# Running the last block of rows of a spectral-mixing and SwiGLU kernel as two half blocks, with the closing stores on two DMA queues

## The chip, the cores and the metric

One Trainium2 chip, one core. The metric is the device time of one launch in microseconds, lower is better. A kernel of 904 us is looked at for an effect of about 1 us. Two lengths are used throughout, both read from a trace:

- **S**: from the start of the first gate matmul of the last block of rows to the start of its last gate matmul (a step's gate is two matmuls; the first of the two is meant);
- **C**: from there to the end of the span.

S + C is all that the change can touch.

The names in the traces: PE runs the matmuls, ACT (ScalarE) the silus, DVE (VectorE) the multiplies (both also copy results), and SP, at the end, only issues stores. PSUM holds the sums of the matmuls, in pieces called banks. A semaphore is a counter that one engine raises and another waits for; a store's completion semaphore tells that its data has landed.

## The reference

In short form:

```python
def reference(x, filt_r, filt_i, w_gate, w_val, w_out, rms_g):   # x: 8 x 3008 x 256, float32
    X = np.fft.rfft(x, axis=1)
    y = np.fft.irfft(X * (filt_r + 1j * filt_i)[None], n=3008, axis=1)
    t = y.reshape(24064, 256)
    tn = t / np.sqrt(np.mean(t * t, axis=-1, keepdims=True) + 1e-6) * rms_g
    g = tn @ w_gate                                              # 256 -> 1536
    return ((g / (1 + np.exp(-g))) * (tn @ w_val)) @ w_out       # 1536 -> 256
```

## The kernel before

The spectral part of a batch runs under the SwiGLU part of the batch before it. The last batch has nothing left to overlap, so the end is SwiGLU alone: for each block of 512 rows, twelve steps (`jt`). A step has four 512-column matmuls (gate and value), a silu on ACT, a multiply on DVE and, two steps later, four 256-column matmuls that add the step's share to the output accumulators. After the twelfth step ACT copies one accumulator bank out of PSUM, DVE the other, and SP issues the stores.

```python
    def gv(b, m, jt):                       # one step: gate, value, silu, multiply
        w = nq(b, m) * P                    # 512 columns
        ...
        for ps, wt in ((pg, wg), (pv, wv)):
            for dt_ in range(2):
                nc.tensor.matmul(ps[:, 0:w], wt[:, dt_, ts(jt, P)], xn[:, dt_, 0:w], ...)
        nc.scalar.activation(out=sg[:, 0:w], in_=pg[:, 0:w], func=AXT.Silu)
        nc.vector.tensor_tensor(out=hh[:, 0:w], in0=pv[:, 0:w], in1=sg[:, 0:w], op=ALU.mult)

    def down(b, m, jt):                     # two steps later
        ...                                 # po: two accumulators, one PSUM bank each
        for s4 in range(n):
            nc.tensor.matmul(po[s4 // 2][:, s4 % 2, :], hh[:, ts(s4, P)], wo[:, jt, :], ...)
        if jt == JT - 1:
            nc.scalar.activation(out=o3[:, 0:2, :], in_=po[0], func=AXT.Copy)
            nc.vector.tensor_copy(out=o3[:, 2:n, :], in_=po[1][:, 0:n - 2, :])

    def o_store(b, m):                      # the last block: 256, 192 and 64 KB
        for h in range(2):
            w = 3 if (m == 5 and (h or b % 2 == 0)) else 4
            lo = h * H + 4 * m
            nc.sync.dma_start(rows[:, lo:lo + w, :], o3[h * 64:h * 64 + 64, 0:w, :])
        if m == 5 and b % 2:                # 64 rows of the batch before ride along
            nc.sync.dma_start(prev[:, H - 1, :], o3[64:P, 3, :])
```

## Time and profile before

| kernel before | |
|---|---|
| time, median of the first three runs | 904.32 us (904.30 to 905.29) |
| span of the profiled run | 903.3 us |
| PE busy | 97% of the span |
| S, C, S + C | 14.52, 8.13, 22.64 us |

Two lines of the page, the busy times and the shares of the chain that ended last:

```profile
PE 878.7 (97%) x6329; PEld 561.0 (62%) x6329; DVE 676.9 (75%) x1075; ACT 619.3 (69%) x1047; POOL 391.4 (43%) x353
...
PE 86%; issue 5%; DMA 3%; DVE 2%; POOL 2%; ACT 2%; SPq 0%; POOLq 0%; ACTq 0%
```

PE bounds the kernel; a change at the end can win only what stands after PE has run dry. That end, from the timeline (start, duration, engine, line, operation, tiles; in brackets the idle time before and what ended it):

```profile
895.65 0.59 PE L420 MATMUL pv<-xn,wv 128*128 128x512 f16 x2
895.85 0.60 ACT L424 ACTIVATE sg<-pg 128x512 f16<-128x512 f32 x1 [0.70 <-PE pg L420]
...
896.08 1.76 PE L437 MATMUL po<-wo,hh 128*128 128x256 f16 x12
896.47 0.69 DVE L425 TENSOR_TENSOR hh<-pv,sg 128x512 f16<-128x512 f32 x1 [0.61 <-ACT sg L424]
...
897.65 0.60 ACT L442 ACTIVATE o<-po 128x512 f32<-128x512 f32 x1 [1.21 <-PE po L437]
897.87 0.69 DVE L443 COPY o<-po 128x512 f32<-128x512 f32 x1 [0.71 <-PE po L437]
898.63 1.11 SPq L452 DMA_DIRECT2D out_dram<-o  x2
899.78 0.61 SPq L456 DMA_DIRECT2D out_dram<-o  x1
```

Three store issues stand in a row until 900.39. The remaining 2.9 us to 903.3 hold no compute. A DMA's line here is only its issue. The Trainium skill, "Perfetto Trace Analysis", section "DMA Instruction — HWDGE (DVE, Sync)", says that the moving of the data lies outside the reported window; this trace agrees, since the third store, issued at 899.785, landed (its completion semaphore's last step in the trace) at 902.355. What SP waits for at the end, from the view of the waits (total us, times, longest):

```profile
SPq L800 <- DMA out_dram<-o: 1.5, 3, 0.9
SPq L800 <- PEq L800: 0.7, 2, 0.5
```

### The profile page before, as it was taken

What the parts mean: (1) busy time and instruction counts of PE and PEld (TensorE: products, weight loads), DVE (VectorE), ACT (ScalarE), POOL (GpSimd) and SP (SyncE); (2) the same over time, 40 slices, a digit from 0 to 9 for tenths busy, and PEclk for the clock granted to TensorE, in tenths of its full rate; (3) what the DMA queues carried; (4) which work ended last, traced back from release to release, by engine and by line L of the source; (5) the groups of instructions that cost most, each with busy time, mean ns of one, the idle gap of its engine ahead of it and who ended that gap; (6) DMA issues with size and microseconds to landing.
All of it is one profiled execution on the core that took longest, in us unless ns stands there. A gap on an engine that the chain in (4) does not pass through costs nothing.

```text
span 903.3 us, 17520 instructions
## 1 busy us (share of the span) xinstructions
PE 878.7 (97%) x6329; PEld 561.0 (62%) x6329; DVE 676.9 (75%) x1075; ACT 619.3 (69%) x1047; POOL 391.4 (43%) x353
## 2 busy tenths in 40 slices
PE   8689999999999999999999999999999999999997
PEld 5565666666666666666666666666666666666564
DVE  7756767789887887888788886887878887555554
ACT  8657666677677766877667766787657765676443
POOL 7832740555635552465325552265514552043300
PEclk9799999999999999999999999999999999999999
DMA  9495734774664437444554347243252332321201
GB/s 199 82 182 159 144 76 164 166 171 79 165 168 116 90 72 213 106 95 113 135 147 111 88 96 193 81 105 82 74 173 71 65 88 54 97 70 48 60 24 46
DMA packets 79747, 100.91 MB, mean 112 GB/s; under 512 B 8097, under 2 KB 56417, under 8 KB 79277
## 3 DMA queue, kind: packets, MB, share of 16 engines
q1 hardware_dynamic: 69276, 83.45, 33.8%
q0 software_dynamic: 10384, 16.35, 11.4%
q8 instruction: 49, 0.80, 0.4%
q14 instruction: 38, 0.30, 0.1%
HBM read 67.67 MB, written 46.78 MB: 127 GB/s over the span
## 4 chain that ended last, share of the span: by engine, by line
PE 86%; issue 5%; DMA 3%; DVE 2%; POOL 2%; ACT 2%; SPq 0%; POOLq 0%; ACTq 0%
PE po L437 25%; PE pg L420 25%; PE pv L420 25%; PE psi L286 3%; PE psb L241 3%; PE psn L318 2%; DMA fr<-in_filt_r_dram 2%; PE psa L204 2%; PE psq L339 1%; DVE o L443 1%; DMA rb<-r_tmp 1%; POOL xc L189 0%; DVE hh L425 0%; ACT fr L478 0%; ACT sg L424 0%
## 5 line engine op out<-in xcount | busy, mean ns | idle before, releaser
L425 DVE TENSOR_TENSOR hh<-pv,sg 128x512 f16<-128x512 f32 (+1 forms) x576 | 391.4, 680 | 203.6 <-ACT sg L424 88.9
L424 ACT ACTIVATE sg<-pg 128x512 f16<-128x512 f32 (+1 forms) x576 | 338.8, 588 | 231.1 <-PE pg L420 223.1
L437 PE MATMUL po<-wo,hh 128*128 128x256 f16 x2256 | 342.3, 272 | 2.3 <-DVE o L443 1.6
L420 PE MATMUL pv<-xn,wv 128*128 128x512 f16 (+1 forms) x1152 | 337.9, 375 | 0.0
L420 PE MATMUL pg<-xn,wg 128*128 128x512 f16 (+1 forms) x1152 | 337.9, 375 | 0.0
L437 PEld LDWEIGHTS <-hh 128*128 128x128 f16 x2256 | 216.5, 98 | 99.2 <-issue 3.6
L277 POOL TENSOR_TENSOR s<-s,s 128x512 f16<-128x512 f16 x96 | 110.5, 1151 | 285.5 <-DVE s L271 199.5
L420 PEld LDWEIGHTS <-wv 128*128 128x128 f16 x1152 | 112.7, 98 | 131.2 <-issue 0.6
L403 POOL TENSOR_TENSOR xn<-y,rb 128x1024 f16<-128x1024 f32 (+1 forms) x45 | 126.1, 2802 | 46.7 <-DMA rb<-r_tmp 32.8
L420 PEld LDWEIGHTS <-wg 128*128 128x128 f16 x1152 | 109.2, 98 | 12.3 <-issue 0.3
L345 POOL TENSOR_TENSOR rho<-u,mhalf 128x4 f32<-128x4 f32 (+1 forms) x48 | 48.9, 1018 | 85.6 <-DVE u L343 85.6
L291 ACT ACTIVATE t<-psi 96x512 f16<-96x512 f32 x112 | 66.3, 592 | 11.8 <-PE psi L286 6.3
L324 ACT ACTIVATE y<-psn,gsb 128x512 f32<-128x512 f32 (+1 forms) x94 | 63.8, 678 | 10.1 <-PE psn L318 3.0
L271 DVE TENSOR_TENSOR s<-psb,fi 64x512 f16<-64x512 f32 x96 | 65.7, 684 | 3.0
L273 DVE SCALAR_TENSOR_TENSOR s<-psb,fi 64x512 f16<-64x512 f32 x96 | 66.5, 693 | 1.3
L247 DVE TENSOR_TENSOR s<-psb,fr 128x512 f16<-128x512 f32 x96 | 65.4, 681 | 0.0
L330 ACT ACTIVATE sq<-psn 128x512 f16<-128x512 f32 (+1 forms) x94 | 54.8, 583 | 0.0
L209 ACT ACTIVATE t<-psa 128x512 f16<-128x512 f32 x70 | 41.8, 597 | 5.6 <-PE psa L204 2.4
L286 PE MATMUL psi<-s,wi 128*128 128x256 f16 x248 | 45.4, 273 | 0.0
L241 PE MATMUL psb<-t,wb 96*128 96x256 f16 x224 | 43.0, 272 | 0.9 <-DVE s L264 0.9
L286 PEld LDWEIGHTS <-wi 128*128 128x128 f16 x248 | 24.2, 98 | 27.0 <-issue 1.9
L318 PEld LDWEIGHTS <-t 128*128 128x128 f16 x368 | 28.5, 99 | 19.9
(97 smaller groups left out, 515.7 us busy)
## 6 DMA issues: line engine op xcount, KB each, us to landing
out_dram<-o SPq DMA_DIRECT2D x84, 256.0 KB
xc<-in_x_dram POOLq DMA_DIRECT2D x56, 192.0 KB, 6.4
z_tmp<-t SPq DMA_DIRECT2D x28, 384.0 KB
t<-z_tmp SPq DMA_DIRECT2D x28, 384.0 KB
g_tmp<-t SPq DMA_DIRECT2D x56, 192.0 KB
rb<-r_tmp SPq DMA_DIRECT2D x41, 256.0 KB
t<-g_tmp SPq DMA_DIRECT2D x21, 384.0 KB
out_dram<-o SPq DMA_DIRECT2D x12, 192.0 KB
```

What stands on the lines that cost most here:

```text
L241: nc.tensor.matmul(ps[:, u, :], w[:, k, :], t, start=True, stop=True)
L247: nc.vector.tensor_tensor(out=s1, in0=ps, in1=f1, op=ALU.mult)
L271: nc.vector.tensor_tensor(out=s2[a], in0=ps[e], in1=f2[e], op=ALU.mult)
L273: nc.vector.scalar_tensor_tensor(out=s2[a], in0=ps[e], scalar=-1.0, in1=f2[e], op0=ALU.mult, op1=ALU.mult)
L277: nc.gpsimd.tensor_tensor(out=s, in0=s1, in1=s2, op=ALU.add)
L286: nc.tensor.matmul(ps[:, u, :], wi_at(q, 2 * i + u), ss[q][:, u, :], start=(q == 0), stop=(q == n - 1))
L291: nc.scalar.activation(out=st[b]["t3"][c][:, 2 * r:2 * r + 2, :], in_=ps[0:KR], func=AXT.Copy)
L403: nc.gpsimd.tensor_tensor(out=xv, in0=yv, in1=rv.unsqueeze(1).to_broadcast([P, 2, n, P]), op=ALU.mult)
L420: nc.tensor.matmul(ps[:, 0:w], wt[:, dt_, ts(jt, P)], xn[:, dt_, 0:w], start=(dt_ == 0), stop=(dt_ == 1))
L424: nc.scalar.activation(out=sg[:, 0:w], in_=pg[:, 0:w], func=AXT.Silu)
L425: nc.vector.tensor_tensor(out=hh[:, 0:w], in0=pv[:, 0:w], in1=sg[:, 0:w], op=ALU.mult)
L437: nc.tensor.matmul(po[s4 // 2][:, s4 % 2, :], hh[:, ts(s4, P)], wo[:, jt, :], start=(jt == 0 and s4 % 2 == 0), stop=(jt == JT - 1 and (s4 ...
```

## The change

The intent is to shorten the tail. The last block runs as two halves of 256 columns, 24 half steps instead of 12. The first half's stores go out under the second half, the second half's chain is shorter, and only 256 KB are left to store at the end, one store of it on ACT's queue beside SP's two.

```diff
-    def gv(b, m, jt):
-        w = nq(b, m) * P
-        xn = st[b]["xn"][m]
+    def cut(b, m, part):
+        return (0, nq(b, m)) if part is None else (2 * part, 2)
+
+    def gv(b, m, jt, part):
+        q0, n = cut(b, m, part)
+        w = n * P
+        xn = st[b]["xn"][m][:, :, q0 * P:q0 * P + w]
 ...
-            po_of[(b, m)] = [psO.tile([P, 2, D], FP32, tag="po%d" % i, name="po%d" % i)
-                             for i in range(2)]
+            po_of[(b, m, part)] = [psO.tile([P, 2, D], FP32, tag="po%d" % i, name="po%d" % i)
+                             for i in range(2) if part is None or i == part]
 ...
+            else:
+                nc.scalar.activation(out=o3[:, 0, :], in_=po[0][:, 0, :], func=AXT.Copy)
+                nc.vector.tensor_copy(out=o3[:, 1, :], in_=po[0][:, 1, :])
 ...
+        if part is not None:
+            lo = 4 * m + 2 * part
+            for h, eng in ((0, nc.scalar), (1, nc.sync)):
+                w = 2 - h * part
+                eng.dma_start(rows[:, h * H + lo:h * H + lo + w, :], o3[h * 64:h * 64 + 64, 0:w, :])
+            if part:
+                prev = ...
+                nc.sync.dma_start(prev[:, H - 1, :], o3[64:P, 1, :])
+            return
 ...
-        items = [(b, m, jt) for b in range(B) for m in range(6) for jt in range(JT)]
+        items = [(b, m, jt, part) for b in range(B) for m in range(6)
+                 for part in ((0, 1) if (b, m) == (B - 1, 5) else (None,)) for jt in range(JT)]
```

More of the change, by code (lines that the diff above doesn't have):

```diff
@@ L419, in gv, with down @@
             for dt_ in range(2):
-                nc.tensor.matmul(ps[:, 0:w], wt[:, dt_, ts(jt, P)], xn[:, dt_, 0:w],
+                nc.tensor.matmul(ps[:, 0:w], wt[:, dt_, ts(jt, P)], xn[:, dt_, :],
                                  start=(dt_ == 0), stop=(dt_ == 1))
         sg = hp.tile([P, 512], FP16, tag="sg", name="sg")
-        hh = hhs[(6 * JT * b + JT * m + jt) % 4]
+        hh = hhs[(6 * JT * b + JT * (m + (part or 0)) + jt) % 4]
         nc.scalar.activation(out=sg[:, 0:w], in_=pg[:, 0:w], func=AXT.Silu)
         nc.vector.tensor_tensor(out=hh[:, 0:w], in0=pv[:, 0:w], in1=sg[:, 0:w], op=ALU.mult)
-        hh_of[(b, m, jt)] = hh
-    def down(b, m, jt):
-        hh = hh_of.pop((b, m, jt))
+        hh_of[(b, m, jt, part)] = hh
+    def down(b, m, jt, part):
+        hh = hh_of.pop((b, m, jt, part))
         if jt == 0:
-            po_of[(b, m)] = [psO.tile([P, 2, D], FP32, tag="po%d" % i, name="po%d" % i)
-                             for i in range(2)]
-        po = po_of[(b, m)]
-        n = nq(b, m)
+            po_of[(b, m, part)] = [psO.tile([P, 2, D], FP32, tag="po%d" % i, name="po%d" % i)
+                             for i in range(2) if part is None or i == part]
+        po = po_of[(b, m, part)]
+        n = cut(b, m, part)[1]
         for s4 in range(n):
@@ L441, in down, with o_store @@
             o3 = late_p["op"].tile([P, 4, D], FP32, tag="o3", name="o3")
-            nc.scalar.activation(out=o3[:, 0:2, :], in_=po[0], func=AXT.Copy)
-            nc.vector.tensor_copy(out=o3[:, 2:n, :], in_=po[1][:, 0:n - 2, :])
-            po_of[(b, m)] = o3
-    def o_store(b, m):
-        o3 = po_of.pop((b, m))
-        rows = out[b * N:(b + 1) * N, :].rearrange("(n2 n1) d -> n2 n1 d", n1=N1)
+            if part is None:
+                nc.scalar.activation(out=o3[:, 0:2, :], in_=po[0], func=AXT.Copy)
+                nc.vector.tensor_copy(out=o3[:, 2:n, :], in_=po[1][:, 0:n - 2, :])
+            else:
+                nc.scalar.activation(out=o3[:, 0, :], in_=po[0][:, 0, :], func=AXT.Copy)
+                nc.vector.tensor_copy(out=o3[:, 1, :], in_=po[0][:, 1, :])
+            po_of[(b, m, part)] = o3
+    def o_store(b, m, part):
+        o3 = po_of.pop((b, m, part))
+        rows = out[b * N:(b + 1) * N, :].rearrange("(n2 n1) d -> n2 n1 d", n1=N1)
+        if part is not None:
[4 more added lines that the diff above has]
+            if part:
+                prev = out[(b - 1) * N:b * N, :].rearrange("(n2 n1) d -> n2 n1 d", n1=N1)
+                nc.sync.dma_start(prev[:, H - 1, :], o3[64:P, 1, :])
+            return
         for h in range(2):
@@ L769 @@
                 if items[i - 2][2] == JT - 1:
-                    stores[i + 1] = items[i - 2][:2]
+                    stores[i + 1] = items[i - 2][:2] + items[i - 2][3:]
             for fn, a in late.get(i, ()):
```

## The prediction

> **What bounds the kernel now.** PE is busy 97% of the 903.3 us span (busy table), and the chain that ended last is 86% PE. In the last block of rows (batch 7, block 5) the timeline shows twelve steps of 1.30 us each: four 512-column matmuls at 0.217 us, then four 256-column down-projection matmuls at 0.109 us, PE never waiting (silu and multiply leave about 1.3 us of slack). So almost the whole time is untouched; only the tail can change.
>
> **The tail before (timeline and chain of waits).** The last gate matmul starts at 895.21. Then silu 0.60 us (from 895.85), multiply 0.69 (from 896.47), four last down matmuls (0.62, from 897.22), DVE copy 0.69 to 898.56, three store issues on the SP queue, 898.63 to 900.39 (0.55, 0.55, 0.61). The fine DMA timeline shows 0.52 MB moving from about 899.7 to 902.0; the span ends at 903.3. Gate matmul to end: 8.1 us.
>
> **What the change does.** It splits the last block in two halves of 256 columns. Matmul columns are unchanged; there are 48 more matmul/weight-load pairs (96 PE rows), 12 more silus and multiplies, one more evacuation pair. The first half's stores run under the second half. The last stores carry 256 KB instead of 512 KB, one issued by ACT, two by SP.
>
> **Costs.**
> - Steps become 0.65 us of PE (six 256-column matmuls, 0.109 each; weight loads, 0.098, still hide, as in the eight back-to-back down matmuls at 896.0).
> - From the 384- and 512-column forms (ACT 491/597 ns, DVE 557/692 ns) I estimate 0.385 us for a half silu and 0.42 for a half multiply; a 256-column DVE copy already exists, 0.414. Both fit under 0.65, so PE should stay the limit.
> - Last gate matmul of the second half starts 0.65 us later than before (23 half steps instead of 11 full). Then the estimated chain: silu at +0.42 to 0.81, multiply to 1.24, two down matmuls to 1.67, copies to 2.09, first store at +2.15 instead of +3.42. Net so far 0.6 us gained.
> - Stores: if SP and ACT issue truly in parallel, the last issue ends at +3.3; if they take turns, at about +3.9; before: +5.2. Data starts about 1.05 us after an issue starts and 1.3 us pass between the last byte and the end. With half the bytes I get +5.55 (parallel) to +5.95 (taking turns) against +8.1.
> - Net: 8.1 - 0.65 - 5.55..5.95 = 1.5 to 1.9 us gained.
> - Given back: ACT's mid-block store issue waits for the DVE copy, then holds ACT's queue about 0.55 us (1.1 if it takes turns with SP), so a silu, then PE, slips 0.1 to 0.5 us. The wait at the entrance to the block (now 0.2 us, the down projection waiting for the previous block's accumulators) stays about 0.2.
>
> The Trainium skill, "DMA: Bandwidth & Descriptors", section "Issuing engines are not separate DMA queues", says a second issuing engine saves only sequencer issue time; I count the second queue as at most 0.55 us. No trace of before shows two queues at once.
>
> All of this is on the critical path. Expected gain 1.3 us (0.15%).
>
> **Prediction: 903.0 us, 902.3 to 904.0.** Faster by over 2%: 0.005; within 2%: 0.99; slower: 0.005.
>
> **What would show it right.** Half steps spaced 0.65 us; half silu near 0.385 us; last copy ending about 0.6 us earlier; 0.26 MB after it; last-store issue to end about 3.5 to 4 us rather than 4.7; one small PE gap after ACT's first store.
>
> **What would make it wrong.** Half steps running slower than 0.65 us (each 0.05 costs 1.2 us) from weight loads, waits or instruction supply; SP and ACT issues excluding each other for longer than one issue; ACT's blocked queue stalling PE by over 0.5 us; a completion tail independent of bytes.

## The result, and the profile after

| | before | after |
|---|---|---|
| time, median of four runs | 904.31 us (903.64 to 905.29) | 905.07 us (904.01 to 905.23) |
| ratio | | 1.0005, 95% interval 0.9988 to 1.0022 |
| span of the profiled run | 903.34 | 903.20 |
| S | 14.52 | 16.08 |
| C | 8.13 | 6.74 |
| S + C | 22.64 | 22.82 |

A ratio is the mean time of one kernel's fast runs over that of the other's fast runs of the same rounds, so it is not quite the ratio of the medians. The times say "same". The traces say more sharply that the end grew by 0.17 us: C shrank by 1.39, S grew by 1.56. The after span is shorter only because its last block began 0.31 us earlier (880.39 against 880.70). That start moves from run to run: in the fourteen traces it lies anywhere from 879.0 to 884.7. S and C do not move: the kernel before, run again in a later job, had S + C = 22.643 both times, and the changed kernel 22.817 and 22.807.

The same lines of the page after:

```profile
PE 877.5 (97%) x6377; PEld 564.1 (62%) x6377; DVE 678.5 (75%) x1088; ACT 621.4 (69%) x1060; POOL 391.4 (43%) x353
...
PE 86%; issue 5%; DMA 3%; ACT 2%; POOL 2%; DVE 2%; SPq 0%; ACTq 0%; POOLq 0%; DVEq 0%
```

The end, from the timeline after:

```profile
896.69 0.38 PE L424 MATMUL pv<-xn,wv 128*128 128x256 f16 x2
...
896.89 0.38 ACT L428 ACTIVATE sg<-pg 128x256 f16<-128x256 f32 x1 [0.27 <-PE pg L424]
896.90 0.62 PE L441 MATMUL po<-wo,hh 128*128 128x256 f16 x4
897.53 0.42 DVE L429 TENSOR_TENSOR hh<-pv,sg 128x256 f16<-128x256 f32 x1 [0.45 <-ACT sg L428]
...
898.01 0.39 PE L441 MATMUL po<-wo,hh 128*128 128x256 f16 x2 [0.48 <-DVE hh L429]
898.44 0.38 ACT L450 ACTIVATE o<-po 128x256 f32<-128x256 f32 x1 [1.17 <-PE po L441]
898.85 0.47 SPq L461 DMA_DIRECT2D out_dram<-o  x1
898.85 0.42 DVE L451 COPY o<-po 128x256 f32<-128x256 f32 x1 [0.90 <-ACT o L450]
899.31 0.49 ACTq L461 DMA_DIRECT2D out_dram<-o  x1
899.40 0.55 SPq L464 DMA_DIRECT2D out_dram<-o  x1
```

Three things are new against before. The last multiply starts 0.25 us after its silu ends (897.27 to 897.53). The DVE copy no longer overlaps the ACT copy but waits for it. And from the last landing (901.85 by the semaphore events) to the end it is 1.35 us, where before it was 0.98. The waits of SP at the end:

```profile
SPq L818 <- DMA out_dram<-o: 1.8, 1, 1.8
SPq L818 <- PEq L818: 0.7, 2, 0.5
```

One wait for landings instead of three: SP met the very last store first. And in the middle, at the border of the halves, ACT's timeline:

```profile
890.39 0.39 ACT L450 ACTIVATE o<-po 128x256 f32<-128x256 f32 x1
890.67 0.38 ACT L428 ACTIVATE sg<-pg 128x256 f16<-128x256 f32 x1
891.26 0.56 ACTq L461 DMA_DIRECT2D out_dram<-o  x1
891.87 0.66 ACT L428 ACTIVATE sg<-pg 128x256 f16<-128x256 f32 x2 [0.82 <-DVE hh L429]
```

ACT stands still for 0.82 us: it waits for the DVE copy, then issues the store, and only then starts the next silu.

### The profile page after: what moved, and what is told of

Read it like the earlier page. It is cut to its first block, busy times and chain, and to the rows that moved or that the text cites. A ratio compares the mean times of both kernels' runs of the same rounds, so it can differ in the third digit from the quotient of the medians.

```text
span 903.2 us, 17669 instructions
## 1 busy us (share of the span) xinstructions
PE 877.5 (97%) x6377; PEld 564.1 (62%) x6377; DVE 678.5 (75%) x1088; ACT 621.4 (69%) x1060; POOL 391.4 (43%) x353
## 4 chain that ended last, share of the span: by engine, by line
PE 86%; issue 5%; DMA 3%; ACT 2%; POOL 2%; DVE 2%; SPq 0%; ACTq 0%; POOLq 0%; DVEq 0%
PE po L441 25%; PE pg L424 25%; PE pv L424 25%; PE psi L286 3%; PE psb L241 3%; PE psn L318 2%; DMA fr<-in_filt_r_dram 2%; PE psa L204 2%; PE psq L339 1%; DVE o L448 1%; DMA rb<-r_tmp 1%; POOL xc L189 0%; ACT sg L428 0%; DVE hh L429 0%; ACT fr L495 0%
## 5 line engine op out<-in xcount | busy, mean ns | idle before, releaser
L429 DVE TENSOR_TENSOR hh<-pv,sg 128x512 f16<-128x512 f32 (+2 forms) x588 | 393.2, 670 | 203.1 <-ACT sg L428 88.9
L428 ACT ACTIVATE sg<-pg 128x512 f16<-128x512 f32 (+2 forms) x588 | 340.8, 580 | 229.8 <-PE pg L424 220.6
L424 PE MATMUL pv<-xn,wv 128*128 128x512 f16 (+2 forms) x1176 | 339.9, 371 | 0.1
L424 PE MATMUL pg<-xn,wg 128*128 128x512 f16 (+2 forms) x1176 | 339.8, 371 | 0.0
L277 POOL TENSOR_TENSOR s<-s,s 128x512 f16<-128x512 f16 x96 | 110.6, 1152 | 285.8 <-DVE s L271 204.1
L424 PEld LDWEIGHTS <-wv 128*128 128x128 f16 x1176 | 114.9, 98 | 129.3 <-issue 0.8
L424 PEld LDWEIGHTS <-wg 128*128 128x128 f16 x1176 | 111.4, 98 | 12.8 <-issue 0.5
```

Source lines behind the costliest of these rows:

```text
L277: nc.gpsimd.tensor_tensor(out=s, in0=s1, in1=s2, op=ALU.add)
```

## The experiments

Theory: halving works as intended, and several small losses, each at a place that can be named, ate the gain. Rival: halving itself costs as much as it saves. Lengths are in us, from each run's trace; "landing" is the last step of a store's completion semaphore, counted from the start of the last gate matmul; "close" is from the last landing to the end of the span.

| run | S | C | S + C | last issue starts | last landing | close |
|---|---|---|---|---|---|---|
| before | 14.518 | 8.125 | 22.643 | 4.571 | 7.141 | 0.984 |
| before, again | 14.516 | 8.127 | 22.643 | 4.571 | 7.143 | 0.984 |
| after | 16.080 | 6.737 | 22.817 | 2.936 | 5.385 | 1.352 |
| after, again | 16.080 | 6.727 | 22.807 | 2.938 | 5.375 | 1.352 |
| one queue | 15.694 | 7.390 | 23.084 | 3.996 | 6.037 | 1.353 |
| second queue only at the end | 15.693 | 6.807 | 22.500 | 2.937 | 5.458 | 1.349 |
| own banks | 16.072 | 6.368 | 22.440 | 2.828 | 5.016 | 1.352 |
| check order | 16.075 | 6.303 | 22.378 | 2.937 | 5.385 | 0.918 |
| shifted DVE stream | 16.072 | 6.527 | 22.599 | 2.715 | 5.180 | 1.347 |
| combined, merged store | 15.692 | 6.147 | 21.839 | 2.482 | 5.229 | 0.918 |
| whole block, two queues | 14.519 | 8.127 | 22.646 | 3.933 | 7.152 | 0.975 |
| whole, half the bytes | 14.517 | 7.240 | 21.757 | 4.259 | 6.256 | 0.984 |
| whole, half the bytes, two queues | 14.517 | 6.788 | 21.305 | 3.620 | 5.804 | 0.984 |
| all losses removed | 15.698 | 5.758 | 21.456 | 2.606 | 4.836 | 0.922 |

### All stores of the halves on SP

```diff
-            for h, eng in ((0, nc.scalar), (1, nc.sync)):
+            for h, eng in ((0, nc.sync), (1, nc.sync)):
```

> The halves kept, every store on SP. Read as two lengths: S, from the first gate matmul of the last block to its last gate matmul (before 14.52 us, after 16.08), and C, from that last gate matmul to the end of the span (before 8.13, after 6.74). Theory (several small losses ate the gain; one is ACT's mid-block store, which keeps ACT from its next silu): S falls by 0.3 to 0.4 to about 15.7, C grows by about 0.4 because three issues of 0.5 us stand in a row again, sum about 22.8 as after. Rival (half steps are simply slower, the store on ACT is harmless): S stays at 16.08.

Measured: S 15.694, C 7.390, sum 23.084; time ratio to before 0.9974 (0.9947 to 1.0002; in this job three of the seven runs of the kernel before lie between 908.8 and 910.2 us, which lowers all four ratios taken with it). S fell by 0.386, as the theory had it: the rival that half steps alone account for S is out. C grew by 0.65, not by 0.4, because the first store, too, now waits for the DVE copy (its issue starts at 2.84 instead of 2.38). So with halves the second queue earns 0.65 us at the end and costs 0.39 us in the middle.

### The second queue only for the last half

```diff
-            for h, eng in ((0, nc.scalar), (1, nc.sync)):
+            for h, eng in ((0, nc.scalar if part else nc.sync), (1, nc.sync)):
```

> First half's stores both on SP, only the last half's first store on ACT. Theory: S about 15.7 (no ACT store in the middle), C as after, 6.7; sum about 22.4, some 0.4 us better than after. Rival (half steps are slower in themselves): S 16.08, sum 22.8.

Measured: S 15.693, C 6.807, sum 22.500; ratio 0.9976 (0.9949 to 1.0002). The loss in the middle is gone and the gain at the end stays (C is 0.07 above after's; ACT's last issue took 0.58 us instead of 0.49). ACT at the border of the halves, from this kernel's timeline:

```profile
890.62 0.39 ACT L428 ACTIVATE sg<-pg 128x256 f16<-128x256 f32 x1 [0.27 <-PE pg L424]
891.06 0.39 ACT L450 ACTIVATE o<-po 128x256 f32<-128x256 f32 x1
891.34 0.38 ACT L428 ACTIVATE sg<-pg 128x256 f16<-128x256 f32 x1
891.93 0.39 ACT L428 ACTIVATE sg<-pg 128x256 f16<-128x256 f32 x1 [0.21 <-PE pg L424]
```

The next silu now waits for PE (0.21 us), which is the harmless direction. S is still 1.175 us over before; that part is in the half steps themselves and is taken up below.

### Two banks for the second half

```diff
+            if part:
+                po_of[(b, m, part)].append(psB.tile([P, 512], FP32, tag="mb", name="po2")
+                                           .rearrange("p (a d) -> p a d", a=2))
 ...
-            nc.tensor.matmul(po[s4 // 2][:, s4 % 2, :], hh[:, ts(s4, P)], wo[:, jt, :],
-                             start=(jt == 0 and s4 % 2 == 0),
+            dst = po[s4][:, 0, :] if part else po[s4 // 2][:, s4 % 2, :]
+            nc.tensor.matmul(dst, hh[:, ts(s4, P)], wo[:, jt, :],
+                             start=(jt == 0 and (part == 1 or s4 % 2 == 0)),
 ...
-                nc.vector.tensor_copy(out=o3[:, 1, :], in_=po[0][:, 1, :])
+                nc.vector.tensor_copy(out=o3[:, 1, :], in_=po[1][:, 0, :] if part else po[0][:, 1, :])
```

> The second half accumulates its two quarters in two PSUM banks (the second one a bank that is free by then), so that the DVE copy need not wait for the ACT copy. Theory (the wait of the DVE copy for the ACT copy is made by the program because both read one accumulator tile): both copies start within 0.1 us of each other, the last copy ends about 0.4 us earlier after the last matmul; since SP is still busy with its first store until then, the last store's issue moves by only 0.05 to 0.2 us and C to 6.5 to 6.7. S unchanged at 16.08. Rival (the two engines cannot read PSUM together): the DVE copy still starts after the ACT copy ends, C unchanged.

Measured: S 16.072, C 6.368; ratio 0.9978 (0.9945 to 1.0011). The two copies in this kernel's timeline:

```profile
898.57 0.38 ACT L454 ACTIVATE o<-po 128x256 f32<-128x256 f32 x1 [1.06 <-PE po L445]
898.68 0.42 DVE L455 COPY o<-po 128x256 f32<-128x256 f32 x1 [0.49 <-PE po L445]
```

They start 0.11 us apart, and DVE is released by PE, not by ACT. The stores of this kernel:

```profile
898.98 0.47 SPq L465 DMA_DIRECT2D out_dram<-o  x1
899.19 0.48 ACTq L465 DMA_DIRECT2D out_dram<-o  x1
899.53 0.55 SPq L468 DMA_DIRECT2D out_dram<-o  x1
```

C fell by 0.37, more than expected (6.5 to 6.7). The last issue moved by only 0.11 us (2.936 to 2.828), within the 0.05 to 0.2 expected; that much comes from ACT's copy, which no longer waits for the second matmul. But ACT's store, which waits for the DVE copy, was issued 0.36 us earlier (2.843 to 2.483), and the last landing moved as far as that, 0.37. So the expectation was wrong in taking the landing to follow the last issue alone. The wait is in the program: in the traces' instruction lists the DVE copy waits for a semaphore that ACT raises with one bank, for one that PE raises with two. The Trainium skill, "PSUM — Partial Sum Buffer", section "PSUM bank collisions raise a hardware error", gives a reason: two engines may not use one bank of the same partitions at the same time. No run here provokes a collision; the runs show the price of avoiding it (0.37 us) and that a second bank lifts it.

### The order of the closing checks

```diff
-            nc.sync.dma_start(rows[:, lo:lo + w, :], o3[h * 64:h * 64 + 64, 0:w, :])
+            eng = nc.gpsimd if (b, m, h) == (7, 3, 1) else nc.sync
+            eng.dma_start(rows[:, lo:lo + w, :], o3[h * 64:h * 64 + 64, 0:w, :])
```

> As after, but one store of an earlier block (7,3) goes through GpSimd's queue, so that the last three stores take the completion semaphores one place earlier in the rotation and the very last one is the last that SP checks before the end, not one of the first. Theory (after the last landing SP still has eight checks of about 0.06 us to do, where before it had four): from the last landing to the end of the span 1.35 us becomes about 1.0, C about 6.4. Rival (the end is only landing plus a fixed barrier): 1.35 us and C 6.74 stay.

Measured: C 6.303, close 0.918 instead of 1.352; ratio 0.9965 (0.9936 to 0.9995). That ratio is more than the tail can explain: S + C is 0.27 us, or 0.03%, under before; the rest I put down to the scatter of what precedes the last block; no run separates it. The waits of SP at this kernel's end:

```profile
SPq L819 <- DMA out_dram<-o: 1.3, 2, 0.9
SPq L819 <- PEq L819: 0.7, 2, 0.5
```

Before the end SP checks every completion semaphore in a fixed order. The DMAs that SP and ACT issue take eight of them in rotation (108, 109 and 113 to 118). In the changed kernel the three last stores fell on semaphores 117, 118 and, starting over, 108, which is looked at second. So SP stood still until the last landing and then walked through the rest of the list; from the events of the changed kernel's trace (start us, what SP checks or does):

```
901.852  last landing (semaphore 108)
901.869  check 108, 105     901.931  109, 104     901.995  113, 103     902.057  114, 102
902.116  115, 101           902.177  116, 100     902.237  117, 99      902.298  118, 107
902.363  112                902.427  drain
```

Some 0.06 us each. One store fewer on this path moves the three to 116, 117 and 118, the first checks are done while the data still flies, and 0.43 us are won with the landing itself unchanged (5.385). The change had added two stores and so moved the last one to a bad place in the rotation.

### DVE's stream shifted by eight instructions

```diff
-        nc.vector.memset(mhalf, -0.5)
+        for _ in range(9):
+            nc.vector.memset(mhalf, -0.5)
```

> As after, with eight more tiny memsets on DVE at the very start, which do nothing but shift DVE's later instructions by eight places in its stream. Theory (the 0.25 us between the end of the last silu and the start of the last multiply, seen in all five split kernels at the same place 1855 in DVE's stream, is instruction supply: it belongs to the place in the stream): the last multiply starts within 0.05 us of the silu's end, C falls from 6.74 to about 6.5, and the gap hides in an earlier step that has slack. Rival (it belongs to the last half step, whatever stands before): the gap stays 0.25 us and C 6.74.

Measured: S 16.072, C 6.527; ratio 1.0005 (0.9982 to 1.0029). The chain that ended last, this kernel's last pieces (start, us, what):

```profile
898.71 0.39 ACT sg L428
899.11 0.02 issue
899.13 0.44 DVE hh L429
...
900.04 0.39 ACT o L450
```

The 0.25 us break before the last multiply is gone from the end, and the trace has it again at the same number, 1855, of DVE's recorded instructions: there now stands a multiply four half steps earlier (each half step has two recorded DVE instructions), which has slack: S stays at 16.07. All nine traces of split kernels have a break of 0.24 to 0.26 us at that number (counted from 0). So it belongs to a place in the stream, not to the half step; C fell by 0.21. The kernel before records only 1836 DVE instructions and never reaches that place; the changed one records 1862. And it is not the only such place: in all fourteen traces, padded or not, the multiplies at numbers 575 and 1727 also start 0.26 us after their silus, where 0.03 is usual. The three places lie 1152 and 128 instructions apart, both multiples of 128. What happens there, the runs do not settle: the nearest recorded instruction fetch of the changed kernel (8 KB) starts at 898.44, after the break.

### All of it combined, with one merged store

The edits of "second queue only at the end" and "two banks", and SP's last two stores written as one, 64 partitions with two rows each:

```diff
+                dst = rows[:, h * H + lo:h * H + lo + 2, :] if not (h and part) else bass.AP(
+                    tensor=out.tensor, offset=out.offset + (b * N + N1 - 1) * D,
+                    ap=[[N1 * D, 64], [-(N + H - 1) * D, 2], [1, D]])
```

> The halves with the three losses removed: second half in two banks, first half stored by SP alone, and the last SP stores merged into one (64 partitions, two rows each, by a negative step in DRAM), so that the last two stores take semaphores that are checked last. Theory: S 15.70, the two last issues start together at about 2.5 us after the last gate matmul and land by about 4.9, landing to end 0.9 to 1.0, C about 5.8 to 5.9; sum 21.5 to 21.6, 1.1 us under before's 22.64; in time about 0.1%, perhaps not to be told from the noise of the runs. Rival (halving cannot pay): sum at or above 22.6.

Measured: S 15.692, C 6.147, sum 21.839; median 907.35 against 905.92 of before on that chip, ratio 1.0006 (0.9980 to 1.0031). The sum beats before by 0.80 us, not by 1.1. The break in DVE's stream is still in this kernel. The merged store is the term that was wrong: its issue took 0.65 us and it landed 2.77 us after its issue began, while ACT's store of as many bytes in pieces twice as long landed after 2.41 (at 4.89, as expected). Why it is slower, no run tells. Three stores in "own banks" had landed 0.2 us earlier than these two.

### The whole block with two queues

```diff
-            nc.sync.dma_start(rows[:, lo:lo + w, :], o3[h * 64:h * 64 + 64, 0:w, :])
+            eng = nc.scalar if (b, m, h) == (7, 5, 0) else nc.sync
+            eng.dma_start(rows[:, lo:lo + w, :], o3[h * 64:h * 64 + 64, 0:w, :])
```

> The last block whole as before; only its first store is issued by ACT, beside SP's two. Theory (most of what the change can win comes from the issues, not from the bytes): S 14.52, issues end about 0.55 us earlier, last landing 0.4 to 0.6 earlier, C 7.5 to 7.7, sum about 22.1, under before and under after. Rival (the 512 KB of the last stores set the landing): C stays at 8.1.

Measured: S 14.519, C 8.127; ratio 1.0008 (0.9986 to 1.0029). The theory fell here, and the rival held. The last store's issue starts 0.64 us earlier, and the last landing is where it was (7.152 against 7.141). The stores in this kernel's timeline:

```profile
898.36 0.47 SPq L453 DMA_DIRECT2D out_dram<-o  x1
898.87 0.59 SPq L457 DMA_DIRECT2D out_dram<-o  x1
```

(ACT's began at 898.38, so the two queues do issue at once.) The Trainium skill, "DMA: Bandwidth & Descriptors", section "Issuing engines are not separate DMA queues", says just this: the engines share the DMA hardware and a second issuer saves only issue time. With 512 KB behind the issues this trace agrees: 0.64 us of issue time saved, nothing gained.

### The whole block, last stores cut to half their bytes

Wrong results. The second kernel also has the edit of the run above.

```diff
             w = 3 if (m == 5 and (h or b % 2 == 0)) else 4
+            w = 2 - h if (b, m) == (7, 5) else w
```

> A wrong result on purpose: the last block whole, all stores on SP as before, but the three last stores write as many bytes as the changed kernel's last three (128, 64 and 64 KB; the other rows of the block are not written). After the run of the whole block with two queues gained nothing (C 8.127 against 8.125), the question is whether bytes alone gain anything. Theory now (the last landing is the later of two things: the last issue plus about 2.4 us, and the time the bytes take; taking away one of the two alone gains little): last issue at 4.57 us after the last gate matmul as before, landing about 7.0, C about 7.9 to 8.0, 0.1 to 0.2 under before. Rival (bytes alone set it): landing about 6.4, C about 7.4.

> A wrong result on purpose: as the half-bytes run, and the first of the three stores is issued by ACT. Theory (both together gain what neither does alone): last issue at 3.93 us, landing 6.3 to 6.5, C 7.3 to 7.5. Rival (something else holds the landing): C above 7.8.

Measured: C 7.240 with one queue, 6.788 with two. My expectation for the first was wrong, for two reasons. The edit does more than intended: stores of two columns need only ACT's copy, so the first issue starts 0.35 us and the last 0.31 us earlier. And the bytes alone do gain: from the start of the last issue to the landing 2.00 us instead of 2.57, so about 0.57 us of the 0.89 are bytes. The second run came out below its range too (7.3 to 7.5), its last issue being 0.31 us early again (3.620), and the theory that neither alone gains is refuted by the first. It shows that the second queue then is worth another 0.45 us, where with all the bytes it was worth nothing. So the bytes come first, and the queue pays only once they are few. Halving the block removes these bytes honestly, at the price in S.

### All losses removed

The edits of "second queue only at the end", "two banks", "check order" and "shifted DVE stream" together, with three last stores.

> All losses removed at once: halves, second half in two banks, ACT store only at the end, one earlier store moved to GpSimd's queue so that the last stores are checked last, and eight tiny memsets so that the break in DVE's stream falls elsewhere; three last stores, not the merged one, which landed 2.77 us after its issue. Theory (losses add): S 15.69, C about 6.37 - 0.22 - 0.43 = 5.7, sum 21.4, 1.2 us under before; in time 0.13%, which these runs will hardly tell from noise. Rival (they overlap): sum above 21.7.

Measured: S 15.698, C 5.758, sum 21.456: 1.19 us under before and 1.36 under the changed kernel; correct. The losses add: 6.737 - 0.210 - 0.369 - 0.434 = 5.724. Of the 1.19 us, 0.06 is the closing checks (0.984 of before against 0.922) and not the halves. Its end in the chain:

```profile
898.85 0.39 ACT sg L428
899.24 0.02 issue
899.27 0.44 DVE hh L429
...
900.18 0.42 DVE o L455
```

In time it is 905.45 us against 906.75 of before on that chip, ratio 0.9991 (0.9972 to 1.0010). The sign fits, but the interval holds 1: eleven runs of the kernel before on that chip lie between 904.22 and 907.81, so 0.13% cannot be told in time. That this version is better is shown for the tail in the trace, not for the launch.

### The two kernels again

> The changed kernel once more, on the chip of the others. Expected: S 16.08 and C 6.74 to 0.05 us, with a different start of the last block (the opening of the kernel varies from run to run by about a microsecond); time within 0.2% of before.

> The kernel before once more, to see how far its tail repeats on another chip: S 14.52 and C 8.13 to 0.05 us; the start of the last block may differ by a few microseconds.

Measured: the changed kernel S 16.080, C 6.727, ratio 1.0013 (0.9990 to 1.0036); the kernel before S 14.516, C 8.127, one time of 904.28. Starts of the last block 879.04 and 879.83. In these traces the tail repeats to 0.01 us from job to job, while the start of the last block moves by 0.9 to 1.4 us; the scatter comes from what precedes it.

## Why the prediction was wrong

The prediction was 903.0 us with a range of 902.3 to 904.0, measured were 905.07. That the time would stay within 2% was right; the forecast gain of 1.3 us did not come. It also counted on 904.3 as a fixed base, though that base scatters by more than the gain; three runs within 1 us had hidden this. What failed is better read from the tail, where the prediction sums to S + C = 21.34 (22.64 - 1.3) and the trace has 22.82. Term by term:

| the step, as the prediction put it | predicted | measured | shown by |
|---|---|---|---|
| "Steps become 0.65 us of PE" | 0.65 | 0.655 | half steps of the timeline |
| "half silu 0.385, half multiply 0.42" | 0.385, 0.42 | 0.384, 0.425 | timeline |
| "Last gate matmul of the second half starts 0.65 us later" | 0.65 | 1.175 | second queue only at the end |
| "a silu, then PE, slips 0.1 to 0.5 us" | 0.1 to 0.5 | 0.39 | the same run against after |
| silu to multiply: no gap ("silu at +0.42 to 0.81, multiply to 1.24") | 1.24 | 1.48 | shifted DVE stream: 0.21 of C |
| "copies to 2.09" | 2.09 | 2.81, with the 0.24 of the row above | own banks: 0.37 of C |
| "1.3 us pass between the last byte and the end" | 1.3 | 1.71 from the end of the last data packet (before: 1.35) | check order: 0.43 of C |
| last gate matmul to end, "+5.55 to +5.95" | 5.75 | 6.74 | all losses removed: 5.758 |

**Right.** That the time would stay within 2% asked little of a change that touches 22.6 us of 904. PE is still the limit inside the half steps, whose length and whose silu and multiply were predicted to 0.01 us. ACT's store in the middle cost what was allowed for. SP and ACT do not take turns at issuing: at 891.26 both issued within 0.01 us, for 0.47 and 0.56 us. The end shrank as a chain: with the losses removed C is 5.758, inside the predicted 5.55 to 5.95.

**Wrong, a mis-sized term in S.** 23 half steps of 0.65 were set against 11 whole ones of 1.30. But the first two half steps still carry the whole down projection of the block before, which lags by two steps: the trace of after has them at 0.87 us, 0.22 more each, with four down matmuls where a half step of its own has two:

```profile
880.39 0.38 PE L424 MATMUL pg<-xn,wg 128*128 128x256 f16 x2
...
880.82 0.60 PE L441 MATMUL po<-wo,hh 128*128 128x256 f16 x4
...
881.26 0.38 PE L424 MATMUL pg<-xn,wg 128*128 128x256 f16 x2
...
881.70 0.60 PE L441 MATMUL po<-wo,hh 128*128 128x256 f16 x4
...
882.13 0.38 PE L424 MATMUL pg<-xn,wg 128*128 128x256 f16 x2
```

Twice 0.22 and twenty times the extra 0.005 make up the difference between 0.65 and 1.175 (0.03 less at the entrance to the block). Said differently: the smaller the last piece, the more of PE's work comes before its start.

**Wrong, three waits that the chain of before did not show.** A chain that was copied from the old trace with shorter durations carried over its releases as well. The copies overlapped before because they used two banks; the half has one (0.37). The last store was checked late before; two more stores turned the rotation (0.43). And a break of 0.25 us at one place of DVE's stream, number 1855, which the kernel before ended short of, fell by chance on the last multiply (0.21). None of them has to come with halving: removed together with ACT's store in the middle they give S + C of 21.456. That this is near the predicted 21.34 is partly luck: S is 0.53 over its predicted term, and the 0.1 to 0.5 allowed for ACT's store is no longer spent.

So where did the gain go? C without the losses is 2.37 us shorter than before; 1.18 of that go to S because of smaller last pieces, and the 1.19 that remain were more than given back: 0.38 in the middle and 0.98 at the end, together 1.36, which leaves the measured loss of 0.17.

## What to carry to other kernels

When the last piece of work is made smaller, recompute when it starts: everything that lags behind is now done before it, and this part of the gain is lost from the outset. Then check each release of the new tail, and not only its durations: which bank each copy reads, which engine a store makes wait, and which place in the order of the closing checks the last store has. Here a second store queue paid only where the bytes behind the issues were few (256 KB and not 512), and only where its engine had nothing else to start.

## What the Trainium skill lacked or had wrong

- No page that I read tells that before the end SP checks the completion semaphores one by one, 0.06 us each, in an order that does not follow the landings; where the last store takes an early place in the rotation, the end came 0.43 us later (close 1.352 against 0.918).
- "Runtime: NRT & Kernel Launch", section "Instruction fetch mechanics", has the fetch hidden behind dispatch. Nine traces had a break of 0.24 to 0.26 us at one place of DVE's stream (1855), which fell on another instruction when eight were put ahead, and all fourteen at numbers 575 and 1727. Whether it is a fetch, no run shows.
- "Perfetto Trace Analysis", section "DMA Instruction — HWDGE (DVE, Sync)", shows an issue that holds the descriptor generator for exclusive use. Here SP's and ACT's issues ran side by side (891.256 to 891.723 and 891.261 to 891.818), 0.47 and 0.56 us long. A wait for the generator would lie inside such a window; ACT's was 0.08 us longer than its shortest here (0.479), so SP and ACT did not take turns for a whole issue, for which the prediction had allowed 0.55 us.
- "DMA: Bandwidth & Descriptors", section "Issuing engines are not separate DMA queues", held where 512 KB stood behind the issues (nothing gained) but gives no rule for when the saved issue time counts: with 256 KB the second queue was worth 0.45 us in a whole block and 0.65 us at the end of the halves.
